# Loading v with a cast through the software DMA queue, in a lightning-attention and gMLP kernel

## The chip, the cores and the metric

The kernel runs on one core of a Trainium2 chip. The metric is the device time of one execution in microseconds (us). Engines: PE (TensorE matmul), PEld (its weight loads), DVE (VectorE), ACT (ScalarE), POOL (GpSimd), SP (SyncE, which here only issues DMAs). "Hardware queue" is the DMA queue that SP issues to, "software queue" the one that POOL issues to. Some executions fall in a slower state; ratios leave those out, while the medians and ranges quoted take in every run. The views count DMA *packets*; the texts, the prediction too, call them descriptors.

## The reference, cut to what matters

```python
# B=4, H=8, S=768, D=64; blocks of 64 tokens
for b in range(nb):                       # lightning attention, decay lam per head
    intra = (q_b @ k_b^T * Dmask) @ v_b
    inter = (q_b * lam_pow) @ kv_state
    out_b = intra + inter
    kv_state = lam_block * kv_state + (k_b * rev_pow)^T @ v_b
x = out as [B, S, H*D]                    # then a gated MLP over the sequence
h = relu(x @ w_in); u, v = halves of h
v_n = layernorm(v)
v_s = w_spatial @ v_n + b_spatial         # mixes the 768 tokens of a batch
y = (u * v_s) @ w_out
```

q, k and v are 6.3 MB each in float32; the weights come to a few MB and are all needed before the first batch can finish.

## The kernel before

There are 12 steps of 256 tokens, three to a batch. A step loads k, q, v, casts them to bf16, transposes, computes scores, the state and the attention output, whose copy **xT** feeds the gMLP matmuls `pv` and `pu`. The last product of a batch, `pvs`, needs all three xT of the batch.

```python
def load_step(n):                         # all on the hardware queue
    ...
    for c in range(2):
        nc.sync.dma_start(out=k_in[:, :, c, :], in_=k[b, :, toks]...)
    nc.sync.dma_start(out=q_in..., in_=q[b, :, toks]...)
    for c in range(2):
        nc.sync.dma_start(out=v_in[:, :, c, :], in_=v[b, :, toks]...)

load_win(DH, DFF)                         # first half of w_in, software queue, with cast
for n in range(1, 4):
    load_step(n)
...
def cast_step(n):
    eng = nc.vector if n < NR else nc.gpsimd
    eng.tensor_tensor(out=kd..., in0=s["k_in"], in1=ldec..., op=ALU.mult)
    nc.scalar.activation(out=qc..., in_=s["q_in"], func=AF.Copy)     # "cast q", ACT
    nc.gpsimd.tensor_copy(out=vc, in_=s["v_in"])                     # "cast v", POOL

def trans_step(n):                        # PE transposes, then kT on ACT, qT on DVE
    ...
    nc.scalar.activation(out=kT, in_=pt[:, 0], func=AF.Copy)

def out_step(n):                          # PE pat, then xT on ACT
    ...
    nc.scalar.activation(out=xT[b][:, r]..., in_=po..., func=AF.Copy)
...
with tc.manual_schedule(engines={PE, Pool}):   # PE and POOL: order as written
    cast_step(0); load_win(0, DH); cast_step(1)
    nc.gpsimd.dma_start(out=wsp_raw, ...)      # w_spatial
    nc.gpsimd.dma_start(out=bsp_bc, ...)       # b_spatial
    nc.gpsimd.dma_start(out=wout_sb, ...)      # w_out
    trans_step(0); scores_step(0); kv_step(0); trans_step(1); load_step(4)
    for n in range(NS):
        if n + 2 < NS: cast_step(n + 2)
        if n + 5 < NS: load_step(n + 5)
        ...
```

One thing in this code matters more than it seems to: only PE and POOL run in the order written. On ACT and DVE a scheduler in the compiler picks the order, and the engine then follows it, waiting for each instruction in turn.

## Time and profile before

| | kernel before |
|---|---|
| time, median of all 4 runs | 184.54 us (183.65 to 187.49) |
| the profiled run | 188.46 us, span 186.7 us, clock 0.963 |
| PE busy | 145.7 us, 78% of the span |
| pv of step 2 starts | 52.95 us |
| second group of pvs starts, PE dense from there | 66.49 us |

The profiled run is one of the longer ones of this kernel: 188.46 us is 2.6% above its fastest, 183.65, and a run is counted as slow from 1.5% on. Its clock (0.963) lies among those of this kernel's fast runs (0.943 to 0.990), so the trace is read here all the same. The prediction below shows the stage table and the wait for v. Two more views of the kernel before are needed to read what follows. First the busy time of each engine from its page (us, share of the span, instructions):

```profile
PE 145.7 (78%) x1540; PEld 96.5 (52%) x1540; DVE 103.4 (55%) x191; ACT 89.1 (48%) x98; POOL 34.8 (19%) x35
```

Then its line in the table of waits for the casts of q (total us, times, longest), and three lines of the timeline of ACT (start us, duration us, engine, line, operation; in brackets the idle time before it and what ended it):

```profile
ACT qc L153 <- DMA q_in<-in_q_dram: 19.0, 7, 7.7
```

```profile
25.96 1.31 ACT L252 ACTIVATE xT<-pat 128x1024 bf16<-128x1024 f32 x1 [3.41 <-PE pat L249]
...
51.58 1.32 ACT L252 ACTIVATE xT<-pat 128x1024 bf16<-128x1024 f32 x1 [0.91 <-PE pat L249]
52.95 1.06 ACT L153 ACTIVATE qc<-q_in 128x1024 bf16<-128x1024 f32 x1
```

These are xT of step 0, xT of step 2 and the cast of q of step 4.

### The profile page before, as it was taken

What the parts mean: (1) busy time and instruction counts of PE and PEld (TensorE: products, weight loads), DVE (VectorE), ACT (ScalarE), POOL (GpSimd) and SP (SyncE); (2) the same over time, 40 slices, a digit from 0 to 9 for tenths busy, and PEclk for the clock granted to TensorE, in tenths of its full rate; (3) what the DMA queues carried; (4) which work ended last, traced back from release to release, by engine and by line L of the source; (5) the groups of instructions that cost most, each with busy time, mean ns of one, the idle gap of its engine ahead of it and who ended that gap; (6) DMA issues with size and microseconds to landing.
All of it is one profiled execution on the core that took longest, in us unless ns stands there. A gap on an engine that the chain in (4) does not pass through costs nothing.

```text
span 186.7 us, 3638 instructions
## 1 busy us (share of the span) xinstructions
PE 145.7 (78%) x1540; PEld 96.5 (52%) x1540; DVE 103.4 (55%) x191; ACT 89.1 (48%) x98; POOL 34.8 (19%) x35
## 2 busy tenths in 40 slices
PE   0005677507979779999997999999799999999980
PEld 0005563305649556655776665575676646565430
DVE  1029993705399853542989747169884722564400
ACT  4244324712677942268775613666722157660051
POOL 4004060006245344060606005020000000000000
PEclk9999996975999979999999999999999999999999
DMA  4999969999999999999998900530000027000035
GB/s 98 218 211 252 205 161 184 199 212 232 199 241 248 200 239 238 221 225 222 330 254 195 252 8 0 208 133 4 0 0 4 2 79 262 0 0 4 0 132 205
DMA packets 68337, 28.36 MB, mean 152 GB/s; under 512 B 50528, under 2 KB 65248, under 8 KB 68320
## 3 DMA queue, kind: packets, MB, share of 16 engines
q1 hardware_dynamic: 65664, 25.17, 56.5%
q0 software_dynamic: 2512, 2.95, 9.6%
q8 instruction: 12, 0.20, 0.5%
q14 instruction: 5, 0.04, 0.1%
q10 hardware_dynamic: 144, 0.00, 0.0%
HBM read 24.78 MB, written 6.29 MB: 166 GB/s over the span
## 4 chain that ended last, share of the span: by engine, by line
PE 54%; SPq 13%; DVE 11%; ACT 9%; DMA 9%; issue 2%; POOL 1%; ACTq 0%; POOLq 0%
PE pvs L307 17%; PE po L322 11%; DMA v_in<-in_v_dram 9%; PE pv L277 8%; PE pu L297 7%; SPq L77 6%; SPq L72 5%; PE pt L163 4%; DVE a L192 3%; PE pvs L309 3%; SPq L74 3%; DVE st L282 3%; ACT vh L280 2%; ACT wt_sb L336 2%; DVE vn L288 2%
## 5 line engine op out<-in xcount | busy, mean ns | idle before, releaser
L307 PE MATMUL pvs<-wt_sb,vn 128*128 128x384 bf16 x192 | 37.8, 331 | 2.1 <-ACT wt_sb L336 2.0
L192 DVE TENSOR_TENSOR a<-pam,amask 128x1024 bf16<-128x1024 f32 x24 | 28.5, 1210 | 6.0 <-PE pam L189 6.0
L154 POOL CAST vc<-v_in 128x1024 bf16<-128x1024 f32 x12 | 12.9, 1074 | 84.0 <-DMA v_in<-in_v_dram 42.7
L252 ACT ACTIVATE xT<-pat 128x1024 bf16<-128x1024 f32 x12 | 15.8, 1320 | 23.7 <-PE pat L249 23.6
L307 PEld LDWEIGHTS <-vn 128*128 128x128 bf16 x192 | 18.9, 99 | 14.9 <-issue 2.5
L297 PE MATMUL pu<-xT,win_sb 128*128 128x256 bf16 x192 | 24.4, 285 | 1.9 <-DVE a L192 1.9
L311 DVE TENSOR_TENSOR gT<-pvs,uT 128x768 bf16<-128x768 f32 x16 | 15.3, 958 | 18.2 <-PE pvs L309 18.1
L277 PE MATMUL pv<-win_sb,xT 128*128 128x512 bf16 x96 | 24.2, 400 | 1.2 <-ACT xT L252 1.2
L322 PE MATMUL po<-wout_sb,gT 128*128 128x512 bf16 x96 | 21.9, 379 | 1.5 <-DVE a L192 1.1
L297 PEld LDWEIGHTS <-win_sb 128*128 128x128 bf16 x192 | 19.2, 102 | 5.7 <-issue 1.8
L153 ACT ACTIVATE qc<-q_in 128x1024 bf16<-128x1024 f32 x12 | 12.7, 1055 | 19.0 <-DMA q_in<-in_q_dram 19.0
L325 ACT ACTIVATE o<-po 128x1024 f32<-128x1024 f32 x12 | 12.3, 1025 | 19.0 <-PE po L322 19.0
L282 DVE BATCH_NORM_STATS2 st<-vh 128x6 f32<-128x512 bf16 x24 | 15.6, 682 | 10.4 <-ACT vh L280 10.3
L163 PE MATMUL pt<-ident,kd 128*128 128x128 bf16 x96 | 8.6, 242 | 15.5 <-DVE kd L150 15.5
L170 DVE TENSOR_TENSOR qT<-pt,lq 128x1024 bf16<-128x1024 bf16 x12 | 8.2, 684 | 18.5 <-ACT kT L168 18.5
L150 POOL TENSOR_TENSOR kd<-k_in,ldec 128x1024 bf16<-128x1024 f32 x9 | 17.1, 1897 | 6.1 <-DMA k_in<-in_k_dram 6.1
L168 ACT ACTIVATE kT<-pt 128x1024 bf16<-128x1024 bf16 x12 | 12.2, 1021 | 11.2 <-PE pt L163 11.2
L280 ACT ACTIVATE vh<-pv 128x1024 bf16<-128x1024 f32 x12 | 12.3, 1024 | 8.8 <-PE pv L277 8.8
L163 PEld LDWEIGHTS <-kd 128*128 128x128 bf16 x96 | 7.2, 110 | 17.4 <-DVE kd L150 15.7
L277 PEld LDWEIGHTS <-xT 128*128 128x128 bf16 x96 | 9.5, 102 | 11.7 <-issue 1.7
L322 PEld LDWEIGHTS <-gT 128*128 128x128 bf16 x96 | 9.2, 98 | 11.9 <-issue 1.0
L299 ACT ACTIVATE uT<-pu 128x1024 bf16<-128x1024 f32 x12 | 12.2, 1020 | 5.9 <-PE pu L297 5.8
(52 smaller groups left out, 146.2 us busy)
## 6 DMA issues: line engine op xcount, KB each, us to landing
k_in<-in_k_dram SPq DMA_DIRECT2D x24, 256.0 KB, 5.8
q_in<-in_q_dram SPq DMA_DIRECT2D x12, 512.0 KB, 6.1
v_in<-in_v_dram SPq DMA_DIRECT2D x24, 256.0 KB, 6.0
out_dram<-o SPq DMA_DIRECT2D x12, 512.0 KB, 3.4
wsp_raw<-in_moe_w_spatial_dram POOLq DMA_DIRECT2D x1, 1152.0 KB, 11.3
win_sb<-in_moe_w_in_dram POOLq DMA_DIRECT2D x2, 512.0 KB, 8.4
wout_sb<-in_moe_w_out_dram POOLq DMA_DIRECT2D x1, 512.0 KB, 14.8
bsp_bc<-in_moe_b_spatial_dram POOLq DMA_DIRECT2D x1, 192.0 KB, 11.7
```

What stands on the lines that cost most here:

```text
L150: eng.tensor_tensor(out=kd.rearrange("p c h d -> p h c d"), in0=s["k_in"], in1=ldec.unsqueeze(2).unsqueeze(3).broadcast_to((P, H, 2, D)), ...
L154: nc.gpsimd.tensor_copy(out=vc, in_=s["v_in"])
L163: nc.tensor.transpose(out=pt[:, j, g, c * P:(c + 1) * P], in_=src[:, c, 2 * g:2 * g + 2, :].rearrange("p h d -> p (h d)"), identity=ident)
L192: nc.vector.tensor_tensor(out=a_sb[:, i].rearrange("p h g c x -> p (h g) c x"), in0=pam.rearrange("p h g c x -> p (h g) c x"), in1=amask[: ...
L252: nc.scalar.activation(out=xT[b][:, r].rearrange("p g (c d m) -> p (g c) m d", c=2, m=2), in_=po.rearrange("p g c (m d) -> p (g c) m d", m ...
L277: nc.tensor.matmul(out=ps[:, j], lhsT=x[:, r, c, j * P:(j + 1) * P], rhs=win_sb[:, c, DH:DFF], start=(c == 0), stop=(c == NCH - 1))
L280: nc.scalar.activation(out=vh[:, pair, :], in_=ps, func=AF.Relu)
L282: nc.vector.bn_stats(out=m["st6"][:, t, :], in_=vh[:, t, :])
L297: nc.tensor.matmul(out=ps[:, f], lhsT=win_sb[:, c, f * P:(f + 1) * P], rhs=x[:, r, c, :], start=(c == 0), stop=(c == NCH - 1))
L307: nc.tensor.matmul(out=ps[:, i, 0:HW_], lhsT=m["vn"][:, s, f * P:(f + 1) * P], rhs=wt_sb[:, s, cols], start=(s == 0), stop=False)
L311: nc.vector.tensor_tensor(out=m["gT"][:, f, :].rearrange("p (i x) -> p i x", i=2), in0=ps[:, :, 0:HW_], in1=m["uT"][:, f, :].rearrange("p ...
L322: nc.tensor.matmul(out=ps[:, j], lhsT=gT[:, c, t * P:(t + 1) * P], rhs=wout_sb[:, c, :], start=(c == 0), stop=(c == NCH - 1))
```

## The change

Its intent: v goes to the software queue, which casts in flight, in one stream with the weights. That frees POOL of 12 casts of v and of waiting for v, and leaves the hardware queue to k and q. The core of the diff:

```diff
+    vin = ctx.enter_context(tc.tile_pool(name="vin", bufs=6))
...
-        for c in range(2):
-            nc.sync.dma_start(out=v_in[:, :, c, :], in_=v[b, :, toks]...)
+    def load_v(n):
+        vc = vin.tile([P, H, 2, D], BF16, tag="vc", name=f"vc_{n}")
+        for c in range(2):
+            nc.gpsimd.dma_start(out=vc[:, :, c, :], in_=v[b, :, rows]...)
...
-        nc.scalar.activation(out=qc..., in_=s["q_in"], func=AF.Copy)
-        nc.gpsimd.tensor_copy(out=vc, in_=s["v_in"])
+        if n == 0:
+            nc.vector.tensor_copy(out=qo, in_=s["q_in"])
+        else:
+            nc.scalar.activation(out=qo, in_=s["q_in"], func=AF.Copy)
...
+        load_v(1)
+        load_win(0, DH)
+        load_v(2)
         cast_step(0)
-        load_win(0, DH)
         cast_step(1)
         nc.gpsimd.dma_start(out=wsp_raw, ...)
         nc.gpsimd.dma_start(out=bsp_bc, ...)
+        load_v(3)
         nc.gpsimd.dma_start(out=wout_sb, ...)
+        load_step(4)
+        load_v(4)
...
             if n + 5 < NS:
                 load_step(n + 5)
+                load_v(n + 5)
```

So the diff also moves the cast of q0 from ACT to DVE, issues `load_step(4)` earlier and gives v buffers of its own (6).

More of the change, by code (lines that the diff above doesn't have):

```diff
@@ L69, in load_step @@
         k_in = fin.tile([P, H, 2, D], FP32, tag="k_in", name=f"k_in_{n}")
-        v_in = fin.tile([P, H, 2, D], FP32, tag="v_in", name=f"v_in_{n}")
         for c in range(2):
@@ L75, in load_step @@
                           in_=q[b, :, toks].rearrange("h (p m) d -> p h (m d)", m=2))
+        st[n] = {"q_in": q_in, "k_in": k_in}
+    def load_v(n):
+        b, r = divmod(n, NR)
+        vc = vin.tile([P, H, 2, D], BF16, tag="vc", name=f"vc_{n}")
         for c in range(2):
-            nc.sync.dma_start(out=v_in[:, :, c, :],
-                              in_=v[b, :, toks][:, c * P:(c + 1) * P].rearrange("h p d -> p h d"))
-        st[n] = {"q_in": q_in, "k_in": k_in, "v_in": v_in}
+            rows = slice(r * T2 + c * P, r * T2 + (c + 1) * P)
+            nc.gpsimd.dma_start(out=vc[:, :, c, :], in_=v[b, :, rows].rearrange("h p d -> p h d"))
+        st[n]["vc"] = vc
     load_step(0)
+    load_v(0)
     ident = const.tile([P, P], BF16)
@@ L147, in cast_step @@
         qc = att.tile([P, 2, H, D], BF16, tag="qc", name=f"qc_{n}")
-        vc = att.tile([P, H, 2, D], BF16, tag="vc", name=f"vc_{n}")
         eng = nc.vector if n < NR else nc.gpsimd
@@ L152, in cast_step @@
                           op=ALU.mult)
-        nc.scalar.activation(out=qc.rearrange("p m h d -> p h m d"), in_=s["q_in"], func=AF.Copy)
-        nc.gpsimd.tensor_copy(out=vc, in_=s["v_in"])
-        s["kd"], s["qc"], s["vc"] = kd, qc, vc
+        qo = qc.rearrange("p m h d -> p h m d")
+        if n == 0:
+            nc.vector.tensor_copy(out=qo, in_=s["q_in"])
+        else:
+            nc.scalar.activation(out=qo, in_=s["q_in"], func=AF.Copy)
+        s["kd"], s["qc"] = kd, qc
     def trans_step(n):
@@ L368 @@
         trans_step(1)
-        load_step(4)
         fills = {0: 1, 1: 2, 2: 5}
```

## The prediction

> **What bounds the kernel now.** I read the stage table first, then the page's slices, the chain of waits and the table of waits.
>
> The stage table (columns: stage, its length, busy time of PE, PEld, DVE, ACT, POOL with counts, granted clock, DMA share, GB/s), cut by me at 26, 52, 66.5 and 182 us:
>
> ```profile
> 0.00:26.00 26.00, 8.00 (x116) 7.04 (x118) 13.13 (x28) 9.07 (x15) 5.92 (x14) 1.00 0.91 187
> 26.00:52.00 26.00, 15.21 (x198) 9.68 (x192) 12.54 (x21) 11.74 (x12) 6.39 (x7) 0.80 1.07 212
> 52.00:66.50 14.50, 11.02 (x153) 9.00 (x154) 13.42 (x26) 12.48 (x13) 6.68 (x5) 1.00 1.18 230
> 66.50:182.00 115.50, 111.45 (x1084) 70.79 (x1083) 64.35 (x120) 55.20 (x60) 15.80 (x12) 0.99 0.46 119
> ```
>
> From 66.5 us on PE is busy 111.45 of 115.5 us; the change takes no work from PE, so nothing is to be had there. Before 66.5 us PE is busy 8.00 + 15.21 + 11.02 = 34.2 us: 32 us are idle, and the DMA engines are full (share 0.91 to 1.18). The head is bound by the order in which inputs land. Its worst spots, in the chain in order of time and in the waits:
>
> ```profile
> 25.91 15.96 DMA v_in<-in_v_dram
> 41.91 0.08 issue
> 42.00 1.05 POOL vc L154
> 43.09 0.43 PE pkv L207 x6
> ```
>
> ```profile
> POOL vc L154 <- DMA v_in<-in_v_dram: 42.7, 6, 14.4
> PE pkv L207 <- POOL vc L154: 8.1, 1, 8.1
> ```
>
> v of step 2 is issued at 25.9 and lands 16 us later; PE stands 8.1 us for it. Why so late is in the DMA view of 29 to 38 us (queue: descriptors, MB, share of engine time):
>
> ```profile
> q0 software_dynamic: 1074, 1.48, 93.3%
> q1 hardware_dynamic: 1074, 0.27, 22.7%
> ```
>
> The software queue is moving weights. Both queues get the same number of descriptors, but a weight descriptor (1536 B written, 3 KB read) takes most of the engine and one of k or v is 256 B. So the hardware queue crawls while the other queue has weights. Alone it runs at 2702 descriptors in the 3 us from 52 on, 900/us; I use 860/us for 256 B ones, 18.6 ns each per engine.
>
> **What the Trainium skill says.** "DMA: Bandwidth & Descriptors", section "Issuing engines are not separate DMA queues": transfers from all queues run on the same 16 engines and interleave. The trace agrees (1074 against 1074), so the change buys no bandwidth. The same page, "Queues, rings and completion order", says the engine takes turns per packet of typically 9 to 17 descriptors; equal packets on both queues would give the 1:1 that the trace counts, and I use the count. Its section "SWDGE vs HWDGE vs iDMA" says that a cast in flight must go through the software queue; the weights before do so. No v with cast has been timed here.
>
> **The change part by part.**
>
> *Removed:* 12 casts of v on POOL, 12.9 us busy (1074 ns each), off the path except where v itself was late; and 24 v transfers (6.3 MB) from the hardware queue. The 8.1 us stall on v of step 2 goes.
>
> *Added:* 24 software issues on POOL. The 768-descriptor issue of wsp took 0.83 us, so about 1 us each, 24 us in all on an engine 19% busy: hidden. The 24,576 descriptors of v stay, each reading 256 B and writing 128; I charge them 18.6 ns as before. Fits to the weights (96 ns for 2 KB read, 134 ns for 3 KB) extrapolate to nearer 29 ns, so this may be too kind.
>
> *Moved, queue:* POOL no longer waits for v between its weight issues. Before, the second w_in went out at 15.1 us and wsp at 25.4, both held back by a cast of v. After, v0, w_in, v1, w_in, v2, wsp, bsp, v3, wout, v4, v5 stand one behind another from about 5 us, so the software queue is never empty before some 55 us, and takes every second descriptor from k and q throughout. Per engine and step: k 128, q 64, v 128 descriptors; w_in 32 each half, wsp 48, bsp 8, wout 32. In pairs: 37 ns (256 B with v), 47 (q with v), 115 (k with w_in), 123 (q with w_in), 153 and 161 (k, q with wsp). The hardware queue starts at 2.8 us, and a landing follows the last descriptor by some 1.5 us. Hand sum of k and q, step by step:
> - q0: 10.9, lands 12.4 (before 11.7).
> - step 1: k1 17.0; q1 with the second w_in, 32 x 0.123 = 3.9: lands 24 (before 18.0).
> - step 2: k2 mostly with v2, 4.2, and 2.3 with wsp: 28.9, lands 30; q2 with wsp and bsp 5.3 + 1.3, lands 38 (before 28.2).
> - step 3: k3 with v3 3.9 and wout 2.7; q3 with the rest of wout and v4 3.7: lands 48.5 (before 45.6).
> - steps 4 to 6: each 6 to 7 us; q6 lands at 68 to 70 (before near 67).
> So v comes early and k and q late; the later q arrives about when it did.
>
> *Moved, order on ACT and DVE:* this is what costs. The order of the changed program shows that on ACT the casts of q move ahead of the work that PE waits for, presumably because the scheduler expects k and q sooner. ACT now runs: cast q1, kT0, cast q2, kT1, cast q3, **xT of step 0**, kT2, vh0, cast q4, xT of step 1, ..., cast q5, cast q6, **xT of step 2**. Before, xT of step 0 came before cast q2 and xT of step 2 before cast q4. Engines run in order, so xT of step 0 now waits for q3 (48.5) and xT of step 2 for q6 (68 to 70). DVE has kd of step 2 (k2, 30 us) ahead of the first a. Also cast q0 stands on DVE ahead of the iota casts that ldec needs: 12.4 + 1.1 + 0.7 puts kd0 at 14 instead of 13.05.
>
> Result: xT0 at 49 + 1 to 50.5 (before 25.96); then pv, scores, out of step 1, kv2, pu, step 3's transposes in some 10 us to out of step 2 at 60; then cast q6 at 69, xT2 to about 71, and pv of step 2 starts at 71. Before it started here:
>
> ```profile
> 52.95 1.90 PE L277 MATMUL pv<-win_sb,xT 128*128 128x512 bf16 x8 [1.16 <-ACT xT L252]
> ```
>
> That is 18 us later. From there to 66.5 before took 13.5 us with 12.5 us of ACT work in it; two casts of q (1.06 each) are already done, and no input is late, so 2 to 4 us come back. Net +14 us in the middle: 184 + 14 = 198 us. PE's work after it is unchanged and dense.
>
> **The rivals.**
> 1. *The intended gain.* If the engines gave k and q more than every second descriptor, or issues of v turned out slow on POOL so that the software queue ran with gaps, q3 and q6 would land in time, the 8.1 us stall would go, and the cold half-clock matmuls (pv at 29.8 us took 3.57 us for 8, later 1.9) would be fewer: 184 - 5 = 179. For it: the stall on v is real and removed. Against it: the 1:1 count, and in 5 to 7 us the hardware queue got even less (126 descriptors beside 301).
> 2. *A wash.* k and q late by some us where before v was, with the ACT order costing only until q3: out of step 2 at 60 instead of 51, and the ACT-limited stage to 66.5 giving half of that back: 184 + 5 = 189. For it: bytes are the same, and q6 lands almost when it did. Against it: cast q6 stands ahead of xT2 in the program.
> 3. *Dearer casts in flight.* At 29 ns a descriptor, eight steps of v add 8 x 128 x 10.4 ns = 10.6 us to the landing of q6: about 208.
>
> **Range and chances.** Main case 198, at about two in three; its own spread is plus or minus 6 (landing of q6, how much comes back). Rival 2 at one in six, rival 1 at one in ten, rival 3 in what remains. Range 186 to 208. Faster by over 2% (under 180.5) 0.09; within 2% 0.13; slower (over 187.9) 0.78.
>
> **What would show it.** In the changed trace: the wait of POOL for v is gone and PE's pkv waits for no v; the DMA view of 10 to 45 us shows equal descriptors on both queues; ACT idles before the casts of q, together well over the 19.0 us of before, the longest ones before casts 3 and 6; xT0 starts near 49 and xT2 near 70; pv of step 2 near 71; from pvs on PE is dense for the same 115 us. The prediction is wrong if the queues don't share 1:1 when both carry 256 B descriptors, if v in the software queue is paced by POOL, or if q6 lands well before 60.

## The result, and the profile after

| | before | after |
|---|---|---|
| median of 4 runs | 184.54 us (183.65 to 187.49) | 205.69 us (205.44 to 205.9) |
| profiled run / its span | 188.46 / 186.7 us | 205.69 / 203.9 us |
| PE busy | 145.7 us (78%) | 144.7 us (71%) |
| cast of q3 / q6 starts | 45.7 / 67.0 us | 45.9 / 67.8 us |
| xT of step 0 / step 2 starts | 25.96 / 51.58 us | 46.89 / 68.74 us |
| pv of step 2 starts | 52.95 us | 70.08 us |

The ratio is 1.1163, 95% interval 1.1114 to 1.1213: 12% slower. Ratios here are the mean time of one kernel's fast runs over the mean of the other's of the same rounds, so they are not quite the ratio of the medians quoted; of the kernel before the run of 187.49 us is left out as slow. In the experiments below, the rounds on one chip often hold several runs of the kernel before that count as slow by their length alone (4 of 7 in those of `a_act` and `b_late`), so a ratio rests there on its fastest few.

The stage table of the kernel after, cut where PE becomes dense (stage, length, busy time and count of PE, PEld, DVE, ACT, POOL, granted clock, DMA share, GB/s):

```profile
0.00:26.00 26.00, 5.31 (x64) 4.62 (x64) 6.59 (x20) 6.95 (x12) 13.98 (x24) 1.00 1.32 177
26.00:52.00 26.00, 8.19 (x86) 5.20 (x88) 10.16 (x15) 5.23 (x6) 6.34 (x6) 0.83 1.43 190
52.00:84.80 32.80, 21.63 (x313) 16.22 (x308) 19.48 (x38) 21.09 (x22) 10.98 (x10) 0.88 1.30 221
84.80:199.00 114.20, 109.58 (x1084) 69.73 (x1083) 65.37 (x120) 53.00 (x58) 12.40 (x9) 1.00 0.28 66
```

The last stage is the same 1084 matmuls in about the same time as before (109.58 against 111.45 us). All of the loss is ahead of it: 84.8 us with 5.31 + 8.19 + 21.63 = 35.1 us of PE work, where before there were 66.5 us with 34.2. What PE was waiting for is in the chain of waits, in order of time (start, duration, what):

```profile
33.03 1.06 ACT qc L162
...
41.80 12.57 DMA q_in<-in_q_dram
54.45 1.06 ACT qc L162
55.51 1.20 ACT xT L260
...
59.81 7.88 DMA q_in<-in_q_dram
67.78 1.06 ACT qc L162
68.83 1.20 ACT xT L260
70.08 3.60 PE pv L285 x8
```

Twice the same three links: a q lands, ACT casts it, ACT makes an xT of an *earlier* step. Those two have nothing to do with each other in the data; they only stand one behind the other on ACT. The timeline of ACT shows the two worst places:

```profile
45.92 1.06 ACT L162 ACTIVATE qc<-q_in 128x1024 bf16<-128x1024 f32 x1 [10.93 <-DMA q_in<-in_q_dram]
46.89 1.29 ACT L260 ACTIVATE xT<-pat 128x1024 bf16<-128x1024 f32 x1
...
67.78 1.06 ACT L162 ACTIVATE qc<-q_in 128x1024 bf16<-128x1024 f32 x1 [4.62 <-DMA q_in<-in_q_dram]
68.74 1.28 ACT L260 ACTIVATE xT<-pat 128x1024 bf16<-128x1024 f32 x1
```

xT of step 0 is stuck behind the cast of q3, xT of step 2 behind that of q6. In the table of waits the idle time of ACT before casts of q has nearly doubled, from 19.0 us:

```profile
ACT qc L162 <- DMA q_in<-in_q_dram: 36.6, 6, 12.0
```

The program itself, before it runs, already shows it. This is the order on ACT as compiled (not a profile; the number is the step of the tile):

```
before: kT0 qc1 kT1 xT0 qc2 kT2 .. xT1 qc3 .. kT3 .. xT2 qc4 .. kT4 uT2 wt wt qc5 xT3 wt qc6
after:  qc1 kT0 qc2 kT1 qc3 xT0 kT2 .. qc4 xT1 .. kT3 .. qc5 qc6 xT2 .. kT4 qc7 uT2 wt wt xT3 wt
```

The rest of the change did what it was meant to: POOL's waits for a cast of v are gone, and the issues of v are cheap. The group line of POOL (count, then busy us in all and mean ns of one):

```profile
L83 POOL DMA_DIRECT2D vc<-in_v_dram x24 | 21.7, 907 | 52.0 <-PE pkv L215 34.3
```

The idle time in that line is POOL running ahead of PE and costs nothing.

### The profile page after: what moved, and what is told of

Its sections match the earlier page's. It is cut to its first block, busy times and chain, and to the rows that moved or that the text cites. A ratio compares the mean times of both kernels' runs of the same rounds, so it can differ in the third digit from the quotient of the medians.

```text
span 203.9 us, 3605 instructions
## 1 busy us (share of the span) xinstructions
PE 144.7 (71%) x1540; PEld 95.8 (47%) x1540; DVE 101.6 (50%) x192; ACT 86.7 (42%) x97; POOL 43.7 (21%) x47
## 3 DMA queue, kind: packets, MB, share of 16 engines
q0 software_dynamic: 27472, 6.10, 32.7%
## 4 chain that ended last, share of the span: by engine, by line
PE 44%; DMA 18%; DVE 13%; ACT 11%; SPq 10%; issue 1%; ACTq 0%
DMA q_in<-in_q_dram 18%; PE pvs L315 15%; PE po L330 10%; SPq L72 8%; PE pv L285 8%; PE pu L305 5%; DVE a L200 4%; DVE st L290 3%; PE pt L171 3%; PE pvs L317 3%; ACT qc L162 2%; ACT wt_sb L344 2%; ACT xT L260 2%; SPq L74 2%; DVE vn L296 1%; DVE gT L319 1%
## 5 line engine op out<-in xcount | busy, mean ns | idle before, releaser
L315 PE MATMUL pvs<-wt_sb,vn 128*128 128x384 bf16 x192 | 36.9, 326 | 1.1 <-ACT wt_sb L344 1.0
L285 PE MATMUL pv<-win_sb,xT 128*128 128x512 bf16 x96 | 25.9, 421 | 15.2 <-ACT xT L260 15.2
L83 POOL DMA_DIRECT2D vc<-in_v_dram x24 | 21.7, 907 | 52.0 <-PE pkv L215 34.3
L162 ACT ACTIVATE qc<-q_in 128x1024 bf16<-128x1024 f32 x11 | 11.6, 1055 | 36.6 <-DMA q_in<-in_q_dram 36.6
L315 PEld LDWEIGHTS <-vn 128*128 128x128 bf16 x192 | 18.6, 98 | 13.4 <-issue 1.3
L305 PE MATMUL pu<-xT,win_sb 128*128 128x256 bf16 x192 | 22.9, 274 | 2.3 <-DVE a L200 2.3
L197 PE MATMUL pam<-qT,kT 64*128 64x128 bf16 x192 | 8.7, 239 | 19.5 <-DVE qT L178 19.5
L305 PEld LDWEIGHTS <-win_sb 128*128 128x128 bf16 x192 | 18.5, 98 | 5.7 <-issue 2.8
L333 ACT ACTIVATE o<-po 128x1024 f32<-128x1024 f32 x12 | 12.3, 1024 | 19.1 <-PE po L330 19.1
L197 PEld LDWEIGHTS <-kT 64*128 64x128 bf16 x192 | 6.6, 105 | 23.4 <-ACT kT L176 18.3
L288 ACT ACTIVATE vh<-pv 128x1024 bf16<-128x1024 f32 x12 | 12.3, 1024 | 10.9 <-PE pv L285 10.3
## 6 DMA issues: line engine op xcount, KB each, us to landing
win_sb<-in_moe_w_in_dram POOLq DMA_DIRECT2D x2, 512.0 KB, 12.4
```

Source lines behind the costliest of these rows:

```text
L83: nc.gpsimd.dma_start(out=vc[:, :, c, :], in_=v[b, :, rows].rearrange("h p d -> p h d"))
L162: nc.scalar.activation(out=qo, in_=s["q_in"], func=AF.Copy)
L285: nc.tensor.matmul(out=ps[:, j], lhsT=x[:, r, c, j * P:(j + 1) * P], rhs=win_sb[:, c, DH:DFF], start=(c == 0), stop=(c == NCH - 1))
L305: nc.tensor.matmul(out=ps[:, f], lhsT=win_sb[:, c, f * P:(f + 1) * P], rhs=x[:, r, c, :], start=(c == 0), stop=(c == NCH - 1))
L315: nc.tensor.matmul(out=ps[:, i, 0:HW_], lhsT=m["vn"][:, s, f * P:(f + 1) * P], rhs=wt_sb[:, s, cols], start=(s == 0), stop=False)
```

## The experiments

Twelve kernels ran. Three theories were put against each other; each expectation says in its own words what it means.

- *Order:* the loss is the order on ACT that the scheduler chose for the changed program.
- *Transfers:* the loss is k and q themselves, which land later because every second descriptor now belongs to v or a weight.
- *Dear casts:* a 256 B descriptor with a cast costs more of the engine than one without.

The tool for the first is an ordering edge: it tells the scheduler that one instruction comes behind another on the same engine, and adds no semaphore and no wait.

```python
def behind(later, earlier):
    tc.add_manual_dep(made[later].ins, made[earlier].ins.name,
                      DependencyInfo(DependencyClass.NoSync, DependencyReason.DATA), reason="order")
```

### The changed kernel with the old order on ACT

```diff
+        behind(('qc', 1), ('kT', 0))
+        behind(('qc', 2), ('xT', 0))
+        behind(('qc', 3), ('xT', 1))
+        behind(('qc', 4), ('xT', 2))
+        behind(('qc', 5), ('wt', 2))
+        behind(('qc', 6), ('wt', 4))
+        behind(('qc', 7), ('kT', 5))
+        behind(('qc', 8), ('qc', 7))
```

> The changed kernel with eight ordering edges on ACT alone, so that each cast of q stands behind the same xT, kT or wt copy as in the kernel before; the transfers and the order on DVE stay as changed. Theory 1 (the casts of q that the scheduler moved ahead of xT turn late landings of q into stalls): q3 and q6 still land near 46 and 68 us, but xT of step 2 runs near 52 instead of 68.7, pv of step 2 starts near 53 instead of 70.1, and the time is 183 to 189 us. Theory 2 (sharing the engines with the software queue costs the time by itself, the order only shows it): the wait moves elsewhere and the time stays at 200 to 206 us.

Measured: 191.51 us (190.41 to 192.26) against 186.56 of the kernel before on the same chip, ratio 1.0363 (1.0246 to 1.048). The order alone brings the ratio from 1.116 to 1.036, with no transfer touched. In the ACT timeline the cast of q3 still starts where it did, near 46 us; but xT of step 2 now waits for PE and not for a q:

```profile
46.70 1.06 ACT L169 ACTIVATE qc<-q_in 128x1024 bf16<-128x1024 f32 x1 [0.98 <-DMA q_in<-in_q_dram]
54.18 1.31 ACT L267 ACTIVATE xT<-pat 128x1024 bf16<-128x1024 f32 x1 [2.08 <-PE pat L264]
```

The wait of ACT for q falls from 36.6 to 13.4 us. The mechanism is right; the time is 2.5 us above the top of what was expected, so 3 to 4% belong to something else (1.036 by the fast runs, 1.027 by the medians). In the chain of waits of this run q3 is still there: 14.0 us of DMA, from 32.65 us on.

### The same with DVE ordered too

```diff
+        behind(('kd', 1), ('qT', 0))
+        behind(('kd', 2), ('a', 1, 1))
```

> As a_act, and on DVE kd of step 1 stands behind qT of step 0 and kd of step 2 behind the masks of step 1, as before. Theory 1: the first 35 us get some us ahead of a_act (pam of step 0 near 16 instead of 20 us), but the transposes of step 3 still wait for q3 at 46 us, so the time is within 1.5 us of a_act. Theory 2: 200 to 206 us.

Measured: 191.76 us, ratio 1.0399 (1.0272 to 1.0525). xT of step 0 comes at 27.28 instead of 33.38 us, xT of step 2 at 53.36 instead of 54.18: what DVE's order cost early is used up by later waits. The time is the same as without these edges.

### The kernel before with the order of the changed one

```diff
+        behind(('kT', 2), ('xT', 0))
+        behind(('kT', 0), ('qc', 1))
+        behind(('kT', 1), ('qc', 2))
+        behind(('xT', 0), ('qc', 3))
+        behind(('xT', 1), ('qc', 4))
+        behind(('xT', 2), ('qc', 6))
+        behind(('qc', 6), ('qc', 5))
+        behind(('uT', 0, 2), ('qc', 7))
```

> The kernel before with edges on ACT alone that give the changed kernel's order: cast q1 before kT0, q2 before kT1, q3 before xT0, q4 before xT1, q5 and q6 before xT2, q7 before uT of step 2; v stays on the hardware queue with its cast on POOL. Theory 1: in the kernel before q3 lands at 45.6 and q6 at 66.9 us, so xT of step 2 runs near 68 to 70 us and the time is 199 to 207 us, although no transfer was changed. Theory 2: 183 to 188 us.

Measured: 202.46 us (200.37 to 203.13), ratio 1.0941 (1.0798 to 1.1085); by the medians it is 1.085. Not one transfer differs from the kernel before, and it is about 9% slower. The ACT timeline has the same picture as that of the changed kernel:

```profile
44.09 1.06 ACT L160 ACTIVATE qc<-q_in 128x1024 bf16<-128x1024 f32 x1 [15.33 <-DMA q_in<-in_q_dram]
45.06 1.29 ACT L259 ACTIVATE xT<-pat 128x1024 bf16<-128x1024 f32 x1
...
63.94 1.06 ACT L160 ACTIVATE qc<-q_in 128x1024 bf16<-128x1024 f32 x1 [2.19 <-DMA q_in<-in_q_dram]
64.91 1.29 ACT L259 ACTIVATE xT<-pat 128x1024 bf16<-128x1024 f32 x1
```

Together: the order by itself makes 1.094, the moved transfers under the old order make 1.036, and the two at once 1.116. They don't add up; presumably because both make ACT wait for the same late q, so that one hides part of the other.

### The kernel before, unchanged, once more

> The kernel before unchanged, for a second profile: the profiled execution of the first took 188.5 us where its runs have a median of 184.5. Both theories: 183 to 186 us here, and the head of the trace (the wait for v of step 2, PE's first dense stretch from pvs at 66.5 us) shows where the other 4 us lay, if this profile falls among the shorter runs.

One run, 188.16 us, state unknown for a single run. It was to show whether the first profile of the kernel before was a long run by chance. It fell among the long ones again, outside the 183 to 186 us that were expected, so it is inconclusive. Over all chips the kernel before scatters from 183.4 to 189.2 us, with one outlier of 236; why, stays open.

### The changed kernel with the weights behind v4 and v5

```diff
-        nc.gpsimd.dma_start(out=wsp_raw, ...)
-        nc.gpsimd.dma_start(out=bsp_bc, ...)
         load_v(3)
-        nc.gpsimd.dma_start(out=wout_sb, ...)
         load_step(4)
         load_v(4)
+        nc.gpsimd.dma_start(out=wsp_raw, ...)
+        nc.gpsimd.dma_start(out=bsp_bc, ...)
...
                 load_v(n + 5)
+            if n == 0:
+                nc.gpsimd.dma_start(out=wout_sb, ...)
```

> The changed kernel with w_spatial and b_spatial issued behind v4 and w_out behind v5, all still in the software queue; the order on ACT and DVE stays that of the changed kernel. Theory 1 (the end is set by q6, which is late because every second descriptor goes to the other queue, whatever its size, until all of it is through): q2 lands near 26 instead of 33 us, q3 near 43 instead of 46, but q6 still at 66 to 69, so xT of step 2 stays near 69 us and the time at 202 to 206 us. Theory 2 (the large weight descriptors in front of k and q are what costs): the 10 us of weights that no longer stand before q3 come off, 194 to 198 us.

Measured: 205.04 us (204.58 to 206.58), ratio 1.0917 (1.081 to 1.1025), against 205.69 for the changed kernel itself. The time is as theory 1 had it, the landings only in part: the cast of q2 starts at 30.47 instead of 33.03 us (26 was expected), that of q3 at 45.90 and so no sooner (43 was expected). The gain on q2 is of no use, since xT of step 2 still stands behind q6:

```profile
67.72 1.06 ACT L162 ACTIVATE qc<-q_in 128x1024 bf16<-128x1024 f32 x1 [2.89 <-DMA q_in<-in_q_dram]
68.68 1.28 ACT L260 ACTIVATE xT<-pat 128x1024 bf16<-128x1024 f32 x1
```

Moving the weights behind v4 and v5 in the software queue decides nothing as long as the order stays.

### The same with the old order

> a_hold with the ordering edges of a_actdve, so that both the late weights and the order of before hold. Theory 1: now q2 and q3 count instead of q6, so holding the weights pays: pv of step 2 near 51 us and the time 185 to 190 us, 2 to 5 us under a_actdve (191.8). Theory 2: as far under a_actdve as a_hold is under the changed kernel.

This is the kernel above with the ten edges of the ordered kernels. Measured: 190.16 us (189.66 to 190.94), ratio 1.0115 (1.0022 to 1.0209): 15 us for ten edges without a wait. The 1.0115 is not what is left of the change's cost, since this kernel also has its weights later. The nearest kernel without the change is `b_hold3` below, with its weights held back too, though not at quite the same places: in the same rounds it took 183.58 us, and 190.16 is 3.6% above that, as much as `a_act` is above the kernel before. That it is the late k and q (q3 is cast at 45.07 us after ACT idled 6.43 us for it, and 18.2 us of DMA for this q stand in the chain of waits) is argued from the timeline, not tested.

### The changed kernel with v in float32 through the software queue

```diff
-        vc = vin.tile([P, H, 2, D], BF16, tag="vc", ...)
+        v_in = vin.tile([P, H, 2, D], FP32, tag="v_in", ...)
...
+    def cast_v(n):
+        vc = att.tile([P, H, 2, D], BF16, tag="vc", ...)
+        nc.gpsimd.tensor_copy(out=vc, in_=st[n]["v_in"])
...
+        behind(('qc', 3), ('kT', 1))
+        behind(('qc', 4), ('kT', 2))
+        behind(('qc', 5), ('kT', 3))
```

> The changed kernel with v still in the software queue at the same places, but moved as fp32 (256 B read and 256 B written) and cast on POOL again; three edges keep the order of the casts of q on ACT. It tells whether the cast in flight slows the engines. If the cast costs nothing (theory 1): where both queues carry 256 B reads, each still runs near 415 descriptors a us, q6 lands within 2 us of 67.7 and the time is 203 to 207 us. If a cast descriptor is dear (the 29 ns of the third rival, theory 3): pairs run faster here, q6 lands 5 us or more earlier, and the time is 195 to 200 us.

Measured: 203.38 us (202.17 to 204.86), ratio 1.0882 (1.081 to 1.0954), with the cast of q6 at 65.69 us: in the range of theory 1, but this settles little. The experiment was to take the cast in flight away and nothing else, and it didn't do only that: the descriptors changed as well. The two queues from the pages, changed kernel first and this one second (descriptors, MB, share of the 16 engines; the first number is the one to look at):

```profile
q0 software_dynamic: 27472, 6.10, 32.7%
```

```profile
q0 software_dynamic: 4432, 9.24, 21.2%
```

With the cast every row of 256 B is a packet of its own; without it v came in 1536 packets of 4096 B. Whether rows were merged or several descriptors went into one packet the view doesn't tell. So this is no clean test of the cast. The answer on its cost comes from the changed kernel. Its DMA view of 22 to 25 us, with k on one queue and v on the other (descriptors, MB, share of the 16 engines; shares of transfers that overlap can pass 100%):

```profile
q1 hardware_dynamic: 1232, 0.33, 79.9%
q0 software_dynamic: 1247, 0.16, 79.8%
```

That is 1247 pairs in 3 us, or 3000 x 16 / 1247 = 38.5 ns per pair and engine, where the prediction charged 37. In 85 to 86 us the software queue, almost alone, moved 968 descriptors. *Dear casts* falls: at 29 ns, one engine would do 34 a microsecond and 16 of them 552. The prediction's 29 ns came from the durations of single weight packets. The packets of v last about as long: a share of 192.6% over 968 of them is 32 ns each. But a share above 100% means that they overlap, so one duration is not what a packet costs.

### The kernel before with its weights later

The remaining runs ask whether the original stall, v of step 2 crawling beside the weights, can be cured without moving v: issue w_spatial, b_spatial and w_out later on POOL. First behind the cast of v of step 2.

```diff
-        nc.gpsimd.dma_start(out=wsp_raw, ...); bsp_bc; wout_sb
...
                 cast_step(n + 2)
+            if n + 2 == 2:
+                nc.gpsimd.dma_start(out=wsp_raw, ...); bsp_bc; wout_sb
```

> The kernel before with w_spatial, b_spatial and w_out issued after the cast of v of step 2 instead of before it; nothing else. Theory 1: v of step 2 lands near 31 instead of 41.9 us and PE's 8.1 us wait for it goes, but k3 and q3 now share with the weights and land near 47, so only part comes back: 180 to 185 us. Theory 2 (bytes before step 3 set the time): 184 to 187 us.

Measured: 189.61 us (187.66 to 190.49), ratio 1.0048 (0.992 to 1.0176): a miss. The profiled run was of the slow state, but the order in it is that of the program. The ACT timeline:

```profile
52.96 1.06 ACT L153 ACTIVATE qc<-q_in 128x1024 bf16<-128x1024 f32 x1 [9.21 <-DMA q_in<-in_q_dram]
53.92 1.28 ACT L252 ACTIVATE xT<-pat 128x1024 bf16<-128x1024 f32 x1
```

The same trap: moving three issues on POOL made the scheduler put the cast of q4 ahead of xT of step 2 on ACT. Then behind the cast of v of step 3 (the number 2 in the diff is a 3):

> As b_hold2, but the three weights are issued after the cast of v of step 3. Theory 1: steps 0 to 3 land by 40 us with the hardware queue alone, pv of step 2 starts near 44 us, w_spatial lands near 52 us while PE works on pv and pu, pvs starts near 58 us: 174 to 180 us, faster than both kernels. Theory 2: 184 to 187 us.

Measured: 183.58 us (183.24 to 183.96), ratio 0.9769 (0.9666 to 0.9872). The direction is right, the size less than expected (174 to 180 us). ACT kept its old order here, and xT of step 2 comes at 43.72 us. But w_out now lies beside v4 and q5, and the third copy of the spatial weights (`wt`, 59.98 us) stands on ACT behind the cast of q5.

To see whether the order ate the gain of the first of the two, the 12th run gave it back the old ACT order:

```diff
+        behind(('qc', 4), ('xT', 2))
+        behind(('qc', 5), ('wt', 2))
```

> The kernel before with w_spatial, b_spatial and w_out issued behind the cast of v of step 2, as in the run before that did not gain, but now with two edges on ACT (cast q4 behind xT of step 2, cast q5 behind the second wt copy), so that ACT has the order of the kernel before. In the run without edges the scheduler had put cast q4 ahead of xT of step 2; ACT waited 9.21 us for q4 there, xT of step 2 began at 53.92 and PE stood 6.18 us for it. Theory 1 (the order on ACT ate the gain): pv of step 2 starts near 49.5 instead of 55.26, and the time is 182 to 185 us, ratio 0.97 to 0.985. Theory 2 (the place of the transfers alone decides): pv of step 2 stays near 55 and the time stays at 187 to 190 us, ratio about 1.00.

Measured: 185.84 us (184.3 to 186.65, 6 runs), ratio 0.9942 (0.9882 to 1.0001) with 187.28 for the kernel before. The order did cost what the timeline said at that place: xT of step 2 starts at 43.62 us instead of 53.92, released by PE's own work, and pv of step 2 at 47.94 instead of 55.26 us.

```profile
43.62 1.31 ACT L259 ACTIVATE xT<-pat 128x1024 bf16<-128x1024 f32 x1 [0.93 <-PE pat L256]
51.91 1.06 ACT L160 ACTIVATE qc<-q_in 128x1024 bf16<-128x1024 f32 x1 [6.99 <-DMA q_in<-in_q_dram]
```

But of the 7.3 us hardly anything, some 1% of the time, reached the end (the 189.61 without the edges is also from another chip): the wait for q4 is still there, only later, and the second group of pvs starts at 65.67 us where the kernel before had it at 66.49. *Order* is right about the stall and too hopeful about its worth, and the 182 to 185 us were missed; presumably the weights beside k, q and v of steps 3 and 4 take the rest.

### The kernel before with its weights in two places

```diff
                 cast_step(n + 2)
+            if n == 1:
+                nc.gpsimd.dma_start(out=wsp_raw, ...); bsp_bc
+            if n == 3:
+                nc.gpsimd.dma_start(out=wout_sb, ...)
```

> The kernel before with w_spatial and b_spatial issued after the cast of v of step 3 (as b_hold3) and w_out after that of step 5. Theory 1: v of step 4 no longer shares with w_out and lands 4 us earlier than the 53.5 of b_hold3, so the first pvs starts some 2 to 4 us earlier: 179 to 183 us. Theory 2: as b_hold3, 183 to 184 us.

Measured: **181.93 us (181.3 to 182.34), ratio 0.9722 (0.969 to 0.9755)** against 186.95 for the kernel before on the same chip: this beats both kernels. That it also beats `b_hold3` is not shown: the two intervals overlap. In its DMA view of 29 to 38 us, the stretch in which the prediction shows 1074 descriptors on each queue, there is one queue:

```profile
q1 hardware_dynamic: 7218, 2.09, 131.9%
```

And pv of step 2 starts 7.4 us sooner than before, at full speed:

```profile
45.53 1.90 PE L277 MATMUL pv<-win_sb,xT 128*128 128x512 bf16 x8 [1.16 <-ACT xT L252]
```

Its ACT order, as compiled, is that of the kernel before in all of the first batch. One more step, two edges that hold the casts of q5 and q6 back behind the third wt copy and xT of step 4:

```diff
+        behind(('qc', 5), ('wt', 4))
+        behind(('qc', 6), ('xT', 4))
```

> As b_split with two ACT edges: cast q5 behind the third wt copy, cast q6 behind xT of step 4, so that no wt copy or xT waits for a q that is needed later. Theory 1: the third wt copy moves from near 60 to near 55 us, and 2 to 4 us come off b_split: 176 to 181 us. Theory 2: no change from b_split.

Measured: 183.51 us (182.4 to 184.7), ratio 0.9811 (0.9752 to 0.9869): a miss. The third wt copy does come 1.3 us sooner (56.23 against 57.54 us) and the second group of pvs too (57.75 against 59.06), but the time is no better. The traces show where the 1.3 us went: into the same trap, a batch later. q8 lands at 80.23 us here and at 77.34 in `b_split`. On ACT its cast (80.27, after 3.73 us of idling) stands ahead of a ready copy `o` of the output, PE waits 4.35 us for that copy, and then runs the next matmuls at half speed (pu 3.09 us for 16, against 1.92). The third pv of that batch starts at 87.63 us instead of 83.83. Why q8 came later was not tested; the casts of q5 and q6 that were held back free their buffers later, which is one candidate.

## Why the prediction was right or wrong

The direction and the main mechanism were right, and the range of 186 to 208 us holds 205.69, but that last is in part luck. The main case was 198 with a spread of 6, so it ended at 204; the range reached 208 only for the rival of dear casts, which the runs refute. The central 198 was 7.7 us too low. By its steps:

**Sharing of the queues: right on the whole.** 1247 against 1232 descriptors where 1:1 was said, and in all of 10 to 45 us 9274 on the software queue against 8785. It is no strict rule: in 5 to 6 us it was 1015 against 164, and in 46 to 49 us 1457 against 1143. Why was not traced.

**Landings: right for q6, which decides most, and too late for the others.** q1 was summed to 24 us and was cast at 19.1, q2 to 38 and 33.0, q3 to 48.5 and 45.9, q6 to 68 to 70 and 67.8. So q3 came 0.2 us later than before where 2.9 was said. A part of the excess is the end of each transfer: the sum has a landing 1.5 us after the last descriptor, and in the two traces a cast of q that waited for its q began 0.4 to 0.9 us after the last packet. The rest was not traced.

**Start: wrong, without effect.** kd0 was to come a microsecond later, at 14 us. It came at 11.06, because q0 landed by 9.9 us and not at 12.4, and its cast on DVE took 0.71 us and not 1.1. PE began 2 us sooner than before (12.35 against 14.33 us) and lost it all behind q3.

**Order on ACT: right, and the main cause.** xT of step 2 was put near 70 us with pv at 71; they came at 68.74 and 70.08. The kernel before with this order alone lost 9.4%. One sign of the prediction failed: ACT was to idle longest before the casts of q3 and q6, and it idled longest before those of q2 (12.0 us) and q3 (10.9), before q6 only 4.6. The place of a wait counted, not its length.

**"2 to 4 us come back" between pv of step 2 and the dense stage: the step that failed.** The stretch to the second group of pvs was 66.49 - 52.95 = 13.54 us before and 84.76 - 70.08 = 14.68 us after. So it grew by 1.1 us, where it was to shrink by 2 to 4. Two casts of q were indeed already done. But one of them (q4) had stood beside a busy PE, where ACT idled 0.64 us after it anyway, and in place of the other (q5) the cast of q7 now stood between kT and uT. And PE was slow: after 7.15 us of idling the eight pv matmuls took 3.60 us, twice the 1.90 of before.

```profile
70.08 3.60 PE L285 MATMUL pv<-win_sb,xT 128*128 128x512 bf16 x8 [7.15 <-ACT xT L260]
```

The Trainium skill, "TensorE: Matmul & The Clock Gate", section "Part 1: The HAM clock gate", says that PE falls to half its clock after an idle window of about 3.4 us and stays there until it has been busy for about as long. The trace agrees here, by 3.60 against 1.90. In the dense stage after it 1.5 us came back (from the second group of pvs to the end of the chain 116.08 us before, 114.63 after), where the prediction had reckoned with none. The traces show it at the start of the stage: the first 27 matmuls took 4.32 us before, at a granted clock of 0.60, and 2.68 us after, at 1.00. In sum the chain shifted by 17.13 + 1.14 - 1.45 = 16.82 us, the span by 17.2, where 14 was said.

**The base: the other half of the miss.** The prediction added a shift read from a trace to the median of the times. The trace of before is of a run of 188.46 us, 4.5 us above the 184 that it started from; from trace to trace the step is 205.69 - 188.46 = 17.2 us. Of the 7.7 us of the miss 3.2 are the shift and 4.5 the base. Why the kernel before scatters by that much and the changed one (205.44 to 205.9) doesn't, is open.

**The rivals.** *The intended gain:* the stall for v is gone, as this rival said, but k and q got no more than half of the turns. *A wash:* the cast of q6 did stand ahead of xT of step 2, as was held against it; without that order, 3 to 4% remain, which is near its 189. *Dear casts:* fell, see above.

## What to carry to other kernels

Where a scheduler picks an engine's order, moving a transfer can change the order on engines that the diff doesn't name: compare the compiled order of every engine before and after, and look for a copy that is ready standing behind a cast whose input is late. Pin it with an ordering edge, which adds no semaphore, before judging the change itself. When two queues share about 1:1 by descriptor, it is the *size* of the other queue's descriptors that starves a queue of small ones; holding big transfers back until the small urgent ones have landed did more here (2.8% faster) than moving the small ones to the other queue.

## What the Trainium skill lacked or had wrong

- "DMA: Bandwidth & Descriptors", section "Queues, rings and completion order", has an engine take turns by packets of typically 9 to 17 descriptors. The runs mostly show near-equal *counts* of packets on two queues, whatever their sizes (1247 and 1232; 421 and 422 while weights moved; 322 and 321 in the run with float32 v), with stretches that differ (1457 and 1143 in 46 to 49 us of the changed kernel). This fits the page, but it doesn't say what follows for bytes and time: in 28 to 32 us of the changed kernel the queue of weights took 88.1% of the engines' time and the queue of k and q 26.3%.
- The same page, section "SWDGE vs HWDGE vs iDMA", says that a cast must go through the software queue, but gives no cost for a cast with small rows. Here 256 B read and 128 B written ran at 38.5 ns a pair with a 256 B copy, and at 968 descriptors a microsecond on 16 engines nearly alone; an issue took POOL 907 ns.
- No page that was read says that with a cast each small row goes as a packet of its own: 27,472 packets on the software queue with it, 4432 without.
- No page that was read warns that the scheduler's order on other engines can follow a moved transfer, nor gives the size of it: 9.4% from the order on ACT alone.
- "TensorE: Matmul & The Clock Gate", section "Part 1: The HAM clock gate", ties the half clock to an idle window of about 3.4 us. Here shorter idling did it in one run and not in another: just ahead of the second group of pvs the kernel before idled 1.96 us and then ran its first 27 matmuls at a clock of 0.60 (4.32 us), while its second profile, `b_same`, idled 1.93 us at the same place and ran them at 1.00 (2.68 us). The page's free-running window may explain it, but no run here shows that.
